# Half a gate product moved from VectorE to ScalarE and GpSimd, and a new written order for a convolution and gating kernel

## Chip, core and metric

The kernel runs on one core of a Trainium2 chip. The metric is the device time of one execution in microseconds; the median of three runs of the kernel before is 351.92 us. Engines are called PE (TensorE matmul), PEld (its weight loads), DVE (VectorE), ACT (ScalarE), POOL (GpSimd) and SP (the queue that issues most transfers).

## The reference

x has shape 8 x 4224 x 192 (batch, sequence, channel), in float32. Two stages follow each other:

```python
# stage 1: causal convolution, 7 taps, one set of softmax weights per head of 24 channels
w = softmax(weight)                       # 8 heads x 7
x = einsum('hk,bskhg->bshg', w, windows(x, 7))
# stage 2: gate and projections
gate_pre = sum(conv_w[k] * shift(x, k) for k in range(5))   # 5 taps, per channel
gate = 1 / (1 + exp(-gate_pre))
out = (gate * (x @ w_val)) @ w_out        # 192 x 192 matrices
```

## The kernel before

**Layout.** Channels lie on partitions. 192 channels are 128 + 64: chunk 1 is 128 channels of two streams side by side (tiles with `128x2x482`, on the page 964 columns), chunk 2 holds the other 64 channels of both streams in one tile of 128 partitions (482 columns). The sequence is cut into 14 groups, and these into 37 steps (0 to 36) of 288, 432, 482, 500 or 244 columns; steps 8 to 34 have 482.

**Stage 1 on PE.** A unit is 4 to 7 windows of a group: small matmuls of x with a banded weight matrix (L323, tile `pc`), whose two results ACT copies into `e` (L335); transfers then scatter rows of `e` into `x1` and `x2`, two groups ahead of use. Tiles of x come in through 8 buffers (L169).

**Stage 2 for a step n.**
- ACT writes tap 0 into an accumulator in PSUM, `pa` (chunk 1) or `pb` (chunk 2) (`gate_open`, L418); DVE adds taps 1 to 4 in place, one instruction per tap (`gate_taps`, L436); ACT writes the sigmoid into `g1` or `g2` (`gate_close`, L449). There is one `pa` and one `pb`: the next step's opening waits for this step's sigmoid.
- x is split into a rounded part `xh` and a rest `xl` (L457, L465 the casts, L458, L466 the subtractions on POOL), and PE forms the value product `v` in three banks: q = 0, 1 for chunk 1, q = 2 for chunk 2 (`diagonal` L492, `columns` L540, `rows` L529, `main` L507).
- DVE multiplies `v` by the gate (`gated`, L558), three instructions per step: two for chunk 1, one for chunk 2. The result is split again into `ph` and `pl`, PE forms the output product `o`, ACT copies it to `ot` (L574) and SP stores it.
- From step 30 on (`WHOLE`), chunk 2 is instead copied to `vt` by ACT (L746) and multiplied by POOL (L750), and parts of the products are done unsplit.

**Order.** Nothing is rearranged: each engine runs its instructions in the order in which the program writes them, and an instruction that waits holds up all behind it on its engine. The order comes from three loops (L630 to L781): steps 0 to 3, 4 to 29, and 30 to 37. In each, PE works at v of step n and o of step n-1, DVE at the taps of step n+1. The five banks for `pc`, `v` and `o` are handed out in turn, and loads of x are issued as the rows of a head are sent.

Of the kernel before, what the change touches and what calls it, by code (L numbers as in the profile page):

```python
# [24 lines left out]
NS = 5  # L25
# [66 lines left out]

UNIT = {2: 4, 3: 6, 5: 7}
# [11 lines left out]
SOON = {2: (0, 0, 1, 1), 3: (1, 2, 2, 2), 4: (3, 3, 3, 4, 4, 4), 5: (5, 5, 6, 6, 7, 7)}  # L105


@with_exitstack
def kernel(
# [21 lines left out]
    ps = ctx.enter_context(tc.tile_pool(name="ps", bufs=5, space=PSUM))  # L131
# [15 lines left out]
    xtiles, loaded = {}, [0]  # L147
# [60 lines left out]

    def zeros(k):
        pw = ps.tile([128, 512], F32, tag="p", name="pw")  # L210
        for i in range(k):
            nc.tensor.matmul(pw[:M, :ZW], lhsT=zero[:, :M], rhs=zero[:, M:], start=True, stop=True)  # L212

# [93 lines left out]
    def conv_unit(u, hold=False):  # L307
# [5 lines left out]
        if ws[0] == (0, 0):  # L313
            es[g, q] = ep.tile([M, 4 * NMAX * WIN], F32, tag="e", name=f"e_{g}_{q}")
        e = es[g, q]
        pc = [ps.tile([128, 512], F32, tag="p", name=f"pc_{u}_{r}") for r in range(2)]
        for k, (hi, j) in enumerate(ws):
# [15 lines left out]

        def evict(r):
            nc.scalar.copy(ev[:, a : a + w, r, :], pc[r][:M, : w * HW].rearrange("p (w t) -> p w t", t=HW))  # L335

        evict(0)
        if hold:
            held.append(lambda: (evict(1), send_rows(g, q, ws, e)))
        else:  # L340
            evict(1)
            send_rows(g, q, ws, e)

    held = []

    def release():
        for f in held:
            f()
        held.clear()

    def send_rows(g, q, ws, e):
        n = NJS[g]
        done = [hi for hi, j in ws if j == n - 1]
        for hi in done:
            h = QUADS[q][hi]
            i, at = home[g, h]
            last = at == len(loads[i][1]) - 1
            if last and g >= BY_POOL:
                load_x(allowed(i))
            scatter(g, h, e[:, hi * n * WIN : (hi + 1) * n * WIN])  # L360
            if last and g < BY_POOL:
                load_x(allowed(i))

    def scatter(g, h, e):
# [11 lines left out]
        def rows(c0, c1):  # L376
            return e[c0 * NS : c1 * NS, :]

        def send(dst, c0, c1, a, b, dma=dma):
            w = NS * (b - a)  # L380
            dma(dst[:, :w].rearrange("p (s t) -> p s t", s=NS), rows(c0, c1)[:, a:b])
# [22 lines left out]
    accs, g1s, g2s, xs, pr, ots, banks, sums = {}, {}, {}, {}, {}, {}, {}, {}  # L404
# [48 lines left out]
    def split1(pool, tag, n, x):  # L453
        m = STEPS[n][2]
        h = pool.tile([128, 2, MB], F32R, tag="h", name=f"{tag}h_{n}")[:, :, :m]
        l = pool.tile([128, 2, MB], F32R, tag="l", name=f"{tag}l_{n}")[:, :, :m]
        nc.scalar.copy(h, x)  # L457
        nc.gpsimd.tensor_tensor(out=l, in0=x, in1=h.bitcast(F32), op=ALU.subtract)  # L458
        return h, l

    def split2(pool, tag, n, x, copy=nc.scalar.copy):
        m = STEPS[n][2]
        h = pool.tile([128, MB], F32R, tag="h2", name=f"{tag}h2_{n}")[:, :m]
        l = pool.tile([128, MB], F32R, tag="l2", name=f"{tag}l2_{n}")[:, :m]
# [394 lines left out]
```

## Time and profile before

| | us |
|---|---|
| three runs, median (lowest, highest) | 351.92 (350.58, 352.64) |
| the profiled execution: its time | 352.94 |
| the profiled execution: its span | 350.8 |
| busy in the span: PE, DVE, ACT, POOL | 336.4, 320.4, 311.0, 252.8 |

The span is what the profiler saw of the core; the time has 2.1 us around it. Busy time of PE is modelled and counts overlapped instructions once. An instruction's duration reaches to its last write, and the next one on the engine may start a little before that, so the distance between two starts can be less than a duration. A name in brackets behind a row says how long the engine stood idle before it and what it waited for.

### The profile page before, as it was taken

To read this page: it belongs to the slowest core of one execution; us is meant where nothing else is said; L and a number is where in the kernel's file an instruction comes from. 1 tells how busy PE (TensorE), PEld (TensorE's weight loads), DVE (VectorE), ACT (ScalarE), POOL (GpSimd) and SP (SyncE) were. 2 spreads that over 40 slices of the span, in tenths; PEclk is the share of its full clock that TensorE was granted. 3 is DMA by queue.
4 is the path that set the end of the run, shared out by engine and by line. 5 is a ranking of instruction groups with operands and counts; after the bars stand their busy time and mean duration, and the time that the engine had idled before them with its cause. 6 is when DMAs were issued, how large, how long until landed. Compare 5 with 4: busy or idle time off the path is not lost.

```text
span 350.8 us, 12959 instructions
## 1 busy us (share of the span) xinstructions
PE 336.4 (96%) x5334; PEld 210.9 (60%) x5334; DVE 320.4 (91%) x427; ACT 311.0 (89%) x544; POOL 252.8 (72%) x195
## 2 busy tenths in 40 slices
PE   8778998999999999999999999999999999999995
PEld 7756655766666666666666666666666665533343
DVE  3898988898999999999999999999999998999950
ACT  7478989787998999999999999999999999999842
POOL 1859855676877888888888888887887877755551
PEclk9999999899999999999999999999999999999998
DMA  7889879899898898898798798798898783442223
GB/s 249 268 212 277 245 235 284 228 274 287 252 277 295 244 295 258 241 277 273 227 283 277 207 286 299 208 283 290 219 293 267 202 314 120 169 152 117 85 86 130
DMA packets 38947, 83.19 MB, mean 237 GB/s; under 512 B 4936, under 2 KB 17008, under 8 KB 38888
## 3 DMA queue, kind: packets, MB, share of 16 engines
q1 hardware_dynamic: 37440, 80.64, 74.9%
q0 software_dynamic: 896, 1.27, 1.5%
q8 instruction: 42, 0.69, 0.9%
q10 hardware_dynamic: 552, 0.46, 0.5%
q14 instruction: 17, 0.14, 0.1%
HBM read 30.06 MB, written 26.00 MB: 160 GB/s over the span
## 4 chain that ended last, share of the span: by engine, by line
PE 84%; DMA 4%; ACT 3%; issue 3%; DVE 2%; SPq 2%; POOL 1%; ACTq 0%; DVEq 0%; POOLq 0%
PE o L507 14%; PE pc L323 14%; PE v L507 11%; PE v L540 9%; PE o L540 8%; PE o L529 6%; PE v L492 6%; PE v L529 5%; PE o L492 5%; DMA x<-e 3%; PE v L500 2%; PE o L521 2%; PE v L521 2%; PE pw L212 1%; DVE pa L436 1%
## 5 line engine op out<-in xcount | busy, mean ns | idle before, releaser
L436 DVE SCALAR_TENSOR_TENSOR pa<-x,cwt,pa 128x964 f32<-128x964 f32 (+4 forms) x148 | 173.4, 1172 | 5.4 <-ACT pa L418 4.9
L458 POOL TENSOR_TENSOR pl<-g,ph 128x964 fp32r<-128x964 f32 (+4 forms) x37 | 79.5, 2150 | 72.1 <-ACT ph L457 63.6
L436 DVE SCALAR_TENSOR_TENSOR pb<-x,cwt,pb 128x482 f32<-128x482 f32 (+4 forms) x142 | 98.6, 694 | 0.3
L558 DVE TENSOR_TENSOR g<-v,g 128x482 f32<-128x482 f32 (+4 forms) x105 | 63.5, 630 | 10.4 <-ACT g L449 3.9
L574 ACT COPY ot<-o 128x482 f32<-128x482 f32 (+4 forms) x111 | 59.7, 547 | 14.7 <-PE o L507 10.2
L323 PE MATMUL pc<-band,x 64*64 64x58 f32 (+1 forms) x3776 | 66.5, 220 | 5.0 <-issue 1.8
L323 PEld LDWEIGHTS pc<-band,x 64*56 64x56 f32 (+1 forms) x3776 | 60.8, 132 | 17.1 <-issue 11.0
L458 POOL TENSOR_TENSOR xl<-x,xh 128x964 fp32r<-128x964 f32 (+2 forms) x32 | 64.3, 2009 | 1.7 <-ACT xh L457 1.6
L335 ACT COPY e<-pc 120x348 f32<-120x348 f32 (+2 forms) x148 | 61.7, 473 | 3.8 <-PE pc L323 3.8
L418 ACT ACTIVATE pa<-x,cwt 128x964 f32<-128x964 f32 (+4 forms) x37 | 38.1, 1029 | 2.7 <-issue 1.6
L457 ACT CAST ph<-g 128x964 fp32r<-128x964 f32 (+4 forms) x37 | 35.8, 966 | 3.8 <-DVE g L558 3.8
L466 POOL TENSOR_TENSOR xl<-x,xh 128x482 fp32r<-128x482 f32 (+2 forms) x30 | 34.2, 1139 | 5.6 <-ACT xh L465 3.6
L449 ACT ACTIVATE g<-pa 128x964 f32<-128x964 f32 (+4 forms) x37 | 34.9, 944 | 3.7 <-DVE pa L436 3.3
L492 PE MATMUL v<-x,wvf 64*64 64x482 f32 (+4 forms) x148 | 37.5, 553 | 0.0
L540 PE MATMUL v<-x,wvf 128*64 128x482 f32 (+4 forms) x148 | 37.4, 572 | 0.0
L492 PE MATMUL o<-g,wof 64*64 64x482 f32 (+4 forms) x148 | 36.5, 567 | 0.8 <-ACT e L335 0.8
L540 PE MATMUL o<-g,wof 128*64 128x482 f32 (+4 forms) x148 | 35.5, 547 | 0.0
L466 POOL TENSOR_TENSOR pl<-g,ph 128x482 fp32r<-128x482 f32 (+2 forms) x30 | 35.2, 1172 | 0.0
L507 PE MATMUL o<-ph,woh 128*128 128x482 f32 (+4 forms) x74 | 31.3, 422 | 0.2 <-ACT ph L457 0.2
L457 ACT CAST xh<-x 128x964 fp32r<-128x964 f32 (+2 forms) x32 | 31.2, 974 | 0.0
L507 PE MATMUL o<-pl,woh 128*128 128x482 f32 (+4 forms) x74 | 27.8, 376 | 1.5 <-POOL pl L458 1.5
L507 PE MATMUL o<-ph,wol 128*128 128x482 f32 (+4 forms) x74 | 27.3, 369 | 0.0
(79 smaller groups left out, 482.8 us busy)
## 6 DMA issues: line engine op xcount, KB each, us to landing
x<-xw SPq DMA_DIRECT2D x72, 300.0 KB
out<-ot SPq DMA_DIRECT2D x27, 723.0 KB
x<-e SPq DMA_DIRECT2D x45, 271.9 KB
x<-xw SPq DMA_DIRECT2D x16, 360.0 KB
x<-e SPq DMA_DIRECT2D x36, 135.9 KB
out<-ot SPq DMA_DIRECT2D x6, 648.0 KB
x<-e SPq DMA_DIRECT2D x20, 163.1 KB
x<-e SPq DMA_DIRECT2D x18, 90.6 KB
```

The lines of the kernel that those rows point to most:

```text
L323: nc.tensor.matmul(pc[r][c0:c1, k * HW : (k + 1) * HW], lhsT=xtiles[i][p, c + c0 : c + c1], rhs=band[p, 4 * q + hi, :], start=True, stop=True,
L335: nc.scalar.copy(ev[:, a : a + w, r, :], pc[r][:M, : w * HW].rearrange("p (w t) -> p w t", t=HW))
L436: nc.vector.scalar_tensor_tensor(out=acc, in0=views(n, k)[i], scalar=cwt[:, i, k : k + 1], in1=acc, op0=ALU.mult, op1=ALU.add,)
L457: nc.scalar.copy(h, x)
L458: nc.gpsimd.tensor_tensor(out=l, in0=x, in1=h.bitcast(F32), op=ALU.subtract)
L466: nc.gpsimd.tensor_tensor(out=l, in0=x, in1=h.bitcast(F32), op=ALU.subtract)
L492: nc.tensor.matmul(dst, lhsT=w22, rhs=x[HALVES[r]], start=True, stop=False)
L507: nc.tensor.matmul(acc, lhsT=a[:, r], rhs=b[:, q], start=(fresh and i == 0), stop=(not fresh and i == 2))
L529: nc.tensor.matmul(acc, lhsT=a[p, r], rhs=b[p], start=(fresh and i == 0), stop=(not fresh and i == 2))
L540: nc.tensor.matmul(acc[HALVES[q if what == "v" else 1 - q]], lhsT=w.f[:, W12 : W12 + 64], rhs=x[:, q], start=False, stop=True)
L558: nc.vector.tensor_tensor(out=v, in0=banks.pop(("v", n, q)), in1=v, op=ALU.mult)
L574: nc.scalar.copy(ots[n][:, q * m : (q + 1) * m], banks.pop(("o", n, q)))
```

## The change

Four things are changed.

1. **Chunk 2 divided by columns.** In steps 6 to 29 DVE multiplies only the left columns of chunk 2 (`gate_left`, token `gd`: 241 of 482, in two steps 216 of 432). ACT copies the right columns of the bank to `vt` (`copy_part`, `vp`), and POOL multiplies them by the gate (`gate_right`, `gq`). As built, the DVE half waits for ScalarE alone, and reads the same bank that the copy reads.
2. **The three loops are replaced by a table.** `ORDER` has a string of tokens for each step; a token is one instruction or a small group, `+1` or `-1` says that it is for the next or the last step, and `A` and `B` are the next tap of `pa` and `pb`. Steps 10 to 25 have one pattern but for the place of the loads of x.
3. **Loads of x** after the start are tokens of their own (`x`), and evictions of `pc` (`e10` and so on) are too. The five banks are taken from a list, the longest free first.
4. **Casts change engine**: in most steps `ph2` is now cast on POOL and `xh2` on ACT; a few of the casts `ph` and `xh` early and late go to POOL. In the whole program ACT has 24 part copies more and 25 casts less, POOL 24 half products and 25 casts more. The numbers of PE, DVE and transfer instructions are the same. `EVEN = 99` leaves `cut` at 64 everywhere, so the windows' matmuls have the shapes of before.

```diff
+SHARE = 241
+ORDER = (
...
+    """
+    dv e11-1 x x ph-1 c2-1 xh2+1 co-1 e20-1 A A e21-1 x pl2-1 cv sB o2-1 ro-1 pl-1 vp gq rv gd A oB+1 B mv0
+    mo0-1 g0 xh+1 mv1 B xl+1 g1 mo1-1 ph2P sA+1 o0-1 oA+2 B xl2+1 o1-1 c1 do e10 A B
+    """,
...
-    ps = ctx.enter_context(tc.tile_pool(name="ps", bufs=5, space=PSUM))
+    ps = ctx.enter_context(tc.tile_pool(name="ps", bufs=1, space=PSUM))
...
+    free = [ps.tile([128, 512], F32, tag=f"p{i}", name=f"p_{i}") for i in range(5)]
+    def take(key):
+        taken[key] = free.pop(0)
+        return taken[key]
+    def give(key):
+        free.append(taken.pop(key))
...
+    def high(p, n, c, copy):
...
+        copy(two[0], x)
+        hs[p, n, c] = x, two
+    def low(p, n, c):
+        x, (h, l) = hs.pop((p, n, c))
         nc.gpsimd.tensor_tensor(out=l, in0=x, in1=h.bitcast(F32), op=ALU.subtract)
...
+    def split_v(n):
+        m = STEPS[n][2]
+        return m - min(SHARE, m // 2)
+    def leave_v(n, other):
+        if (other, n) in did:
+            drop("v", n, 2)
+    def copy_part(n):
+        a = split_v(n)
+        vts[n] = vp.tile([128, MB], F32, tag="vt", name=f"vt_{n}")[:, : STEPS[n][2] - a]
+        nc.scalar.copy(vts[n], banks["v", n, 2][:, a:])
+        leave_v(n, "gd")
+    def gate_left(n):
+        a = split_v(n)
+        v = g2s[n][:, :a]
+        nc.vector.tensor_tensor(out=v, in0=banks["v", n, 2][:, :a], in1=v, op=ALU.mult)
+        leave_v(n, "vp")
+    def gate_right(n):
+        v = g2s[n][:, split_v(n) :]
+        nc.gpsimd.tensor_tensor(out=v, in0=vts.pop(n), in1=v, op=ALU.mult)
...
+    for n, tokens in enumerate(ORDER):
+        for t in tokens.split():
+            if t in "AB":
+                tap(t)
+                continue
+            if t == "x":
+                load_x(loaded[0] + 1)
+                continue
+            i = max(t.rfind("+"), t.rfind("-"))
+            step(t[:i] if i > 0 else t, n + (int(t[i:]) if i > 0 else 0))
```

Three places show what moves. The first is DVE in the middle of the program, one step's worth; `pa_18` is the accumulator of chunk 1 of step 18, `g2_18` the gate of chunk 2, and two names with different last numbers are different tiles. Before, from the second half of step 18:

```order
L436 SCALAR_TENSOR_TENSOR pb_18_3151<-x2_7_2312,cwt_158,pb_18_3151 128x482
L436 SCALAR_TENSOR_TENSOR pa_19_3203<-x1_7_2311,cwt_158,pa_19_3203 128x2x482
L436 SCALAR_TENSOR_TENSOR pb_18_3151<-x2_7_2312,cwt_158,pb_18_3151 128x482
L436 SCALAR_TENSOR_TENSOR pa_19_3203<-x1_7_2311,cwt_158,pa_19_3203 128x2x482
L558 TENSOR_TENSOR g2_18_3297<-v_18_2_3283,g2_18_3297 128x482
L436 SCALAR_TENSOR_TENSOR pa_19_3203<-x1_7_2311,cwt_158,pa_19_3203 128x2x482
L436 SCALAR_TENSOR_TENSOR pb_19_3304<-x2_7_2312,cwt_158,pb_19_3304 128x482
L436 SCALAR_TENSOR_TENSOR pa_19_3203<-x1_7_2311,cwt_158,pa_19_3203 128x2x482
L436 SCALAR_TENSOR_TENSOR pb_19_3304<-x2_7_2312,cwt_158,pb_19_3304 128x482
L558 TENSOR_TENSOR g1_18_3201<-v_18_0_3337,g1_18_3201 128x482
L558 TENSOR_TENSOR g1_18_3201<-v_18_1_3338,g1_18_3201 128x482
```

Now, the step before it (`p_0` to `p_4` are the five banks):

```order
L597 SCALAR_TENSOR_TENSOR pa_18_2908<-x1_7_2194,cwt_162,pa_18_2908 128x2x482
L597 SCALAR_TENSOR_TENSOR pb_17_2880<-x2_7_2195,cwt_162,pb_17_2880 128x482
L597 SCALAR_TENSOR_TENSOR pa_18_2908<-x1_7_2194,cwt_162,pa_18_2908 128x2x482 x2
L725 TENSOR_TENSOR g2_17_2998<-p_0_121,g2_17_2998 128x241
L597 SCALAR_TENSOR_TENSOR pa_18_2908<-x1_7_2194,cwt_162,pa_18_2908 128x2x482
L597 SCALAR_TENSOR_TENSOR pb_18_3020<-x2_7_2195,cwt_162,pb_18_3020 128x482
L699 TENSOR_TENSOR g1_17_2905<-p_3_124,g1_17_2905 128x482
L597 SCALAR_TENSOR_TENSOR pb_18_3020<-x2_7_2195,cwt_162,pb_18_3020 128x482
L699 TENSOR_TENSOR g1_17_2905<-p_2_123,g1_17_2905 128x482
```

The product of chunk 2 is half as wide; the two products of chunk 1 stand apart with a tap between them; and two taps of the same `pa` stand next to each other (`x2`), where before a tap of `pb` or a product always stood between two taps of one accumulator.

The second place is ACT in the same stretch. Before:

```order
L449 ACTIVATE g1_17_3054<-pa_17_2905 128x2x482
L418 ACTIVATE pa_18_3056<-x1_7_2311,cwt_158 128x2x482
L335 COPY e_8_1_2952<-pc_44_0_3066 120x7x58
L335 COPY e_8_1_2952<-pc_44_1_3067 120x7x58
L335 COPY e_8_1_2952<-pc_45_0_3101 120x6x58
L457 CAST ph_16_3138<-g1_16_2903 128x2x482
L449 ACTIVATE g2_17_3142<-pb_17_3004 128x482
L335 COPY e_8_1_2952<-pc_45_1_3102 120x6x58
L418 ACTIVATE pb_18_3151<-x2_7_2312,cwt_158 128x482
L457 CAST xh_18_3157<-x1_7_2311 128x2x482
L574 COPY ot_16_3166<-o_16_2_3131 128x482
L465 CAST ph2_17_3168<-g2_17_3142 128x482
```

Now, up to the sigmoid that ends `pa` of the next step:

```order
L503 COPY e_8_1_2814<-p_1_122 120x7x58
L624 CAST ph_16_2953<-g1_16_2761 128x2x482
L624 CAST xh2_18_2980<-x2_7_2195 128x482
L503 COPY e_8_1_2814<-p_4_125 120x6x58
L503 COPY e_8_1_2814<-p_3_124 120x6x58
L610 ACTIVATE g2_17_2998<-pb_17_2880 128x482
L736 COPY ot_16_3000<-p_2_123 128x482
L719 COPY vt_17_3009<-p_0_121 128x241
L579 ACTIVATE pb_18_3020<-x2_7_2195,cwt_162 128x482
L624 CAST xh_18_3030<-x1_7_2194 128x2x482
L610 ACTIVATE g1_18_3045<-pa_18_2908 128x2x482
```

The cast `ph2` has left ACT and `xh2` has come; the part copy `vt` stands behind the sigmoid of `g2` and an output copy, and it is what the half product of `g2_17` on DVE waits for.

The third place is DVE in step 1. Before:

```order
L436 SCALAR_TENSOR_TENSOR pa_1_440<-x1_0_179,cwt_158,pa_1_440 128x2x288
L436 SCALAR_TENSOR_TENSOR pb_1_478<-x2_0_180,cwt_158,pb_1_478 128x288 x2
L558 TENSOR_TENSOR g2_1_602<-v_1_2_606,g2_1_602 128x288
L436 SCALAR_TENSOR_TENSOR pa_2_598<-x1_1_298,cwt_158,pa_2_598 128x2x432
L558 TENSOR_TENSOR g1_1_596<-v_1_0_620,g1_1_596 128x288
```

Now:

```order
L597 SCALAR_TENSOR_TENSOR pa_1_428<-x1_0_183,cwt_162,pa_1_428 128x2x288
L597 SCALAR_TENSOR_TENSOR pb_1_464<-x2_0_184,cwt_162,pb_1_464 128x288
L699 TENSOR_TENSOR g2_0_462<-p_2_123,g2_0_462 128x288
L597 SCALAR_TENSOR_TENSOR pb_1_464<-x2_0_184,cwt_162,pb_1_464 128x288
L699 TENSOR_TENSOR g1_1_595<-p_1_122,g1_1_595 128x288
L699 TENSOR_TENSOR g1_1_595<-p_0_121,g1_1_595 128x288
L699 TENSOR_TENSOR g2_1_627<-p_3_124,g2_1_627 128x288
```

Between the last tap of `pb_1` and the product that needs its sigmoid, `g2_1`, there was nothing; now two products stand there.

## Rows read from the trace of the kernel before

**Rows 1.** The page: busy us, share of the span and instructions of each engine.
```profile
PE 336.4 (96%) x5334; PEld 210.9 (60%) x5334; DVE 320.4 (91%) x427; ACT 311.0 (89%) x544; POOL 252.8 (72%) x195
```
**Rows 2.** Stretches: length, then busy PE, PEld, DVE, ACT, POOL; clock; DMA.
```profile
17.00:111.00 94.00, 86.62 (x1612) 57.86 (x1612) 85.02 (x116) 82.37 (x153) 67.99 (x60) 0.98 0.89 258
111.00:290.00 179.00, 179.00 (x3029) 114.63 (x3030) 179.00 (x224) 170.34 (x284) 143.36 (x100) 1.00 0.87 264
290.00:337.00 47.00, 46.97 (x350) 20.66 (x346) 42.82 (x52) 43.69 (x73) 29.36 (x19) 1.00 0.32 115
```
**Rows 3.** Timeline of DVE over one step: start us, length us, instruction, count.
```profile
181.41 1.25 DVE L558 TENSOR_TENSOR g<-v,g 128x482 f32<-128x482 f32 x2
...
186.15 0.65 DVE L558 TENSOR_TENSOR g<-v,g 128x482 f32<-128x482 f32 x1
186.72 1.22 DVE L436 SCALAR_TENSOR_TENSOR pa<-x,cwt,pa 128x964 f32<-128x964 f32 x1
187.85 0.72 DVE L436 SCALAR_TENSOR_TENSOR pb<-x,cwt,pb 128x482 f32<-128x482 f32 x1
...
190.28 0.66 DVE L558 TENSOR_TENSOR g<-v,g 128x482 f32<-128x482 f32 x1
```
**Rows 4.** Timeline of DVE late: three taps of one accumulator in a row.
```profile
301.70 3.75 DVE L436 SCALAR_TENSOR_TENSOR pa<-x,cwt,pa 128x964 f32<-128x964 f32 x3
```
**Rows 5.** Groups by form: busy us, mean ns of one, idle before.
```profile
L558 DVE TENSOR_TENSOR g<-v,g 128x482 f32<-128x482 f32 x76 | 48.0, 658 | 2.2 <-PE v L507 1.8 <-PE o L540 0.3
...
L574 ACT COPY ot<-o 128x244 f32<-128x244 f32 x3 | 1.1, 363 | 1.2 <-PE o L507 0.7 <-PE o L540 0.4
...
L558 DVE TENSOR_TENSOR g<-v,g 128x244 f32<-128x244 f32 x3 | 1.2, 412 | 2.9 <-ACT g L449 1.8 <-PE v L500 1.1
```
**Rows 6.** Timeline of ACT over one step in the middle.
```profile
190.01 0.98 ACT L449 ACTIVATE g<-pa 128x964 f32<-128x964 f32 x1
191.03 1.07 ACT L418 ACTIVATE pa<-x,cwt 128x964 f32<-128x964 f32 x1
192.04 1.19 ACT L335 COPY e<-pc 120x348 f32<-120x348 f32 x3
193.11 1.01 ACT L457 CAST ph<-g 128x964 fp32r<-128x964 f32 x1
194.02 0.57 ACT L449 ACTIVATE g<-pb 128x482 f32<-128x482 f32 x1
194.49 0.49 ACT L335 COPY e<-pc 120x406 f32<-120x406 f32 x1
...
196.36 0.57 ACT L574 COPY ot<-o 128x482 f32<-128x482 f32 x1
196.81 0.61 ACT L465 CAST ph<-g 128x482 fp32r<-128x482 f32 x1
```
**Rows 7.** Who waited for whom, DVE: us in total, times, longest.
```profile
DVE pa L436 <- ACT pa L418: 4.9, 6, 1.6
DVE g L558 <- ACT g L449: 3.9, 6, 1.8
DVE g L558 <- PE v L507: 2.8, 5, 1.5
```
**Rows 8.** Timeline of DVE in step 1, the place shown above.
```profile
28.25 1.08 DVE L436 SCALAR_TENSOR_TENSOR pb<-x,cwt,pb 128x288 f32<-128x288 f32 x2
30.41 0.46 DVE L558 TENSOR_TENSOR g<-v,g 128x288 f32<-128x288 f32 x1 [1.08 <-ACT g L449]
```
**Rows 9.** Timeline of PE: windows and the next `columns`, middle, then late.
```profile
190.75 1.68 PE L323 MATMUL pc<-band,x 64*64 64x58 f32 x102
...
193.49 1.03 PE L540 MATMUL v<-x,wvf 128*64 128x482 f32 x4
...
305.93 0.92 PE L323 MATMUL pc<-band,x 64*64 64x58 f32 x48
...
307.73 1.03 PE L540 MATMUL v<-x,wvf 128*64 128x482 f32 x4
```

More of the change, by code (lines that the diff above doesn't have):

```diff
@@ L91, with cut @@
 PER_LOAD = {2: 2, 3: 2, 5: 1}
+EVEN = 99
+SHARE = 241
+def cut(g, h):
+    return M // 2 if g >= EVEN and h < 5 else 64
 UNIT = {2: 4, 3: 6, 5: 7}
@@ L313, in conv_unit @@
         if ws[0] == (0, 0):
[L314 to L316 removed]
+            es[g, q] = ep.tile([128, 4 * NMAX * WIN], F32, tag="e", name=f"e_{g}_{q}")
+        pc = [take(("c", u, r)) for r in range(2)]
         for k, (hi, j) in enumerate(ws):
@@ L615 @@
     gate_open(0, 1)
-    split(0)
+    high("x", 0, 2, nc.scalar.copy)
+    low("x", 0, 2)
+    high("x", 0, 1, nc.scalar.copy)
+    low("x", 0, 1)
     gate_taps(0, 0, 1, 2)
@@ L781, with tap @@
-    assert not held
+    by_order.append(True)
+    unit_of = {}
+    u = done[0]
+    for n in range(N):
+        unit_of[n] = list(range(u, min(u + todo[n], len(units))))
+        u += len(unit_of[n])
+    assert u == len(units)
+    line = {
+        c: [(n, k) for n in range(1, N) for k in range(2 if i and n in SUMMED else 1, KG)]
+        for i, c in enumerate("AB")
+    }
+    def tap(c):
+        if line[c]:
+            n, k = line[c].pop(0)
+            gate_taps(n, "AB".index(c), k, k + 1)
@@ new lines, in evicts, with step @@
+    def evicts(n, i, r):
+        if i <= len(unit_of[n]):
+            evict(unit_of[n][i - 1], r)
+    def step(t, n):
+        copy = nc.gpsimd.tensor_copy if t[-1] == "P" else nc.scalar.copy
+        t = t.removesuffix("P")
+        p, c = t[0], 2 if t[-1] == "2" else 1
+        assert ok(n) and (t, n) not in did, (t, n)
+        did.add((t, n))
+        if t in ("dv", "do"):
+            diagonal(t[1], n)
+        elif t in ("cv", "co"):
+            columns(t[1], n)
+        elif t in ("rv", "ro"):
+            rows(t[1], n)
+        elif p == "m":
+            main(t[1], n, int(t[2]))
+        elif p == "c":
+            if int(t[1]) <= len(unit_of[n]):
+                conv_unit(unit_of[n][int(t[1]) - 1])
+        elif p == "e":
+            evicts(n, int(t[1]), int(t[2]))
+        elif t in ("g0", "g1", "g2"):
+            gated(n, int(t[1]))
+        elif t == "vp":
+            copy_part(n)
+        elif t == "gd":
+            gate_left(n)
+        elif t == "gq":
+            gate_right(n)
+        elif t == "vt":
+            copy_v(n)
+        elif t == "gp":
+            gate_v(n)
+            did.add(("g2", n))
+        elif t in ("o0", "o1", "o2"):
+            project(n, int(t[1]))
+        elif p == "s" and t != "su":
+            gate_close(n, "AB".index(t[1]))
+        elif t in ("oA", "oB"):
+            gate_open(n, "AB".index(t[1]))
+        elif t == "su":
+            gate_sum(n)
+        elif p in "xp" and (n < PLAIN if p == "x" and c == 1 else n < WHOLE or c == 1):
+            if t[1] == "h":
+                high(p, n, c, copy)
+            else:
+                low(p, n, c)
```

434 lines of the change are left out of this document (204 added, 230 removed).

## The prediction

> **What bounds the kernel now.** I read the busy shares first [rows 1]: PE 96%, DVE 91%, ACT 89%. A share is a mean over stages, so the stretches came next [rows 2]. From 111 to 290 us PE and DVE are busy for all of the 179.00 us; ACT stands idle for 8.66, POOL for 35.64. From 17 to 111 DVE is idle for 94.00 - 85.02 = 8.98 us and PE for 7.38. From 290 to 337 PE is full again (46.97 of 47.00) and DVE idle for 4.18. PE's clock is 0.98 to 1.00 throughout, so it does not enter.
>
> Which of two full engines sets the pace? The timeline of DVE over one step [rows 3] tells it from starts: the pair of products starts at 181.41 and the next at 190.28, so a step takes 8.87 us and no start is late. A product takes 186.72 - 186.15 = 0.57 us to the next start, a tap of `pa` 187.85 - 186.72 = 1.13. PE is hardly looser. From the start of a step's windows to `columns` it takes 193.49 - 190.75 = 2.74 us for 102 passes [rows 9]; late it takes 307.73 - 305.93 = 1.80 for 48. At the rate of the 102 (1.68 us, 16 ns a pass) 54 passes fewer are 0.89 us less, which makes 1.85: at most about 0.1 us of a step on PE is waiting. So a faster DVE can win only some 0.1 us per step before PE takes over, unless PE's own order gets shorter.
>
> **The change part by part.** All numbers of instructions are counted in the two orders.
>
> *Halved products.* A product of 482 columns lasts 658 ns and one of 244 lasts 412 [rows 5]: 1.03 ns a column. 241 columns fewer save 0.25 us, so the start-to-start time falls from 0.57 to 0.32. There are 22 of these and two with 216 columns fewer (0.22): 5.9 us less on DVE.
>
> *Taps of one accumulator side by side.* Three taps of `pa` in a row last 3.75 us in all [rows 4]; without the last one's 1.23 that is 1.26 from start to start, 0.13 more than the 1.13 of a tap that something else follows. A tap reads what the one before it wrote, and beside its neighbour nothing covers the end of that write. Before, 15 pairs of `pa` taps stand so, now 49: 34 x 0.13 = 4.4 us more. Pairs of `pb` go from 9 to 12, which at the same 0.13 is 0.4. DVE therefore keeps only 5.9 - 4.8 = 1.1 us of work less, spread unevenly. Steps 10 to 27 have one such pair each and one halved product: 0.25 - 0.13 = 0.12 us per step. The late steps, from 28, have 7 + 5 pairs more and two halved products: 1.1 us more. Steps 0 to 9 come out even.
>
> *Middle.* By DVE a step falls from 8.87 to 8.75. ACT must still fit. It is busy 170.34 of 179.00 us, which is 8.44 of each 8.87. The part copy adds 0.25 (half of 482 columns at 1.03, the 363 ns of a 244-column copy [rows 5] being the bound above); the casts that change places are equal in size. That makes 8.69. POOL has room: 143.36 of 179.00. A halved product on DVE now stands behind ACT's part copy; queued behind it on DVE are the last tap of `pa`, and so the next sigmoid on ACT. The ring this closes, in starts from [rows 6]: sigmoid 1.02, output copy 0.45, opening 1.01, output copy 0.45, four evictions of 0.36 (three from 192.04 to 193.11), cast `ph` 0.91, cast `xh2` at most 0.61, sigmoid of `g2` 0.47, output copy 0.45, part copy 0.36: 7.17 on ACT; then 0.32 and one tap of 1.22 on DVE: 8.71. It fits by 0.04. Three engines within 0.1 us of one another will not all meet their best, so I take 0.10 of the 0.12: 18 steps give 1.8 us.
>
> *Early.* What DVE waits for is mostly ACT [rows 7]: reopened accumulators 4.9 us, sigmoids 3.9, v products 2.8, in the whole run. In step 1 two taps of `pb` are followed at once by the product that needs the sigmoid of that `pb`: 1.08 us idle [rows 8]. The new order puts two products between. From the last tap of `pa` to the first of the next step it now has six instructions instead of three in step 1, three for two in step 2, four for two in step 3. Such waits can be hidden; the longest, 1.6 us, comes when a new group's data are first used, and order alone does not bring those sooner. What goes is between nothing and 7.4 us, since PE idles for no more than that there and has no work less. The waits that got longer cover are nearer to half than to either end: I take 3.4 us.
>
> *Late.* DVE's 1.1 us lie within its 4.18 us of idle, and PE is full: nothing. If that cover is gone, 1.1 us.
>
> *Loads and evictions as tokens, banks from a list.* In the middle a tile of x is still issued about five heads ahead and its buffer was freed some heads ago; the work of those heads hides it. Were it late, PE would wait for it as single windows may anywhere. I cost it at nothing.
>
> Sum: 1.8 + 3.4 = 5.2 us. The profiled execution took 352.94 (span 350.8 and 2.1 around it), which gives 347.7. It stands 1.0 above the median of the runs, 351.92; against that the forecast is 346.7.
>
> **Rivals.**
>
> *A, the waits really go (slack everywhere).* The taps' neighbourhood costs nothing because the copy or a product's end was the true limit there, and PE's second windows block hides its `diagonal`. Then a middle step loses all of 0.25, 18 x 0.25 = 4.5, and early all of PE's 7.4: 11.9 us, 340.0. For it: PE's late steps are shorter than the middle ones [rows 9]. Against it: the 1.26 was read where DVE had no other work.
>
> *B, PE is the bound and the early waits only move.* PE's 179.00 of 179.00 speaks for it, and each early wait on a new group comes back elsewhere. Then the middle gives nothing and early at most 1.5: 350.4 to 352.5, about 351.5.
>
> *C, slower: the halved product waits for the part copy.* The place is the product of chunk 2 on DVE in each of the 18 middle steps. DVE has two taps, 1.26 + 1.13 = 2.39 us, between the last tap of `pb` and this product; ACT must do a sigmoid, an output copy and the part copy in them (0.47 + 0.45 + 0.36 = 1.28), but five older instructions stand ahead on ACT. It decides as soon as the ring is over 8.87. The ring has 8.71 without any stall, and ACT's present idle is 8.66 us in 179.00, 0.43 per step; if that stays inside the ring it is 9.14, 0.27 per step over before: 4.9 us more in the middle, with half of the early gain, 1.7, against it: 355.1. Were nothing on ACT overlapped, more still; but [rows 6] shows starts 0.1 us ahead of ends throughout.
>
> The Trainium skill (PSUM — Partial Sum Buffer, section PSUM bank collisions raise a hardware error) speaks for this wait: two engines that touch the same bank and the same 32 partitions at once collide, reads against reads too. By it the two halves cannot be read side by side, and the wait of the one for the other cannot be taken out of the order. No run here shows a collision; by the rule the price would be C's, without it the product would wait only for the sigmoid and C's chance would fall.
>
> **How the numbers follow.** The forecast has 0.52: between the middle at 0.05 and at 0.15 per step and early at 1 to 6 us it reaches from 343.5 to 350.5. A has 0.13, B 0.19, C 0.16. The range for 8 in 10 leaves out the low half of A and the upper part of C: 341 to 354.5. About 0.5% (1.8 us) is what a measurement of this kernel tells from no change, so faster means under 350.2 and slower over 353.7. Faster: 0.50 + 0.13 + a little of B, 0.65. Same: most of B and the edges of the others, 0.21. Slower: most of C, 0.14.
>
> **What would show it.** DVE's busy time should fall by about 1 us, not 6, and pairs of `pa` taps in the middle should start 1.26 apart; 1.13 would speak for A. The step in the middle, from one pair's place to the next, should be 8.75 to 8.8. Idle of DVE from 17 to 111 us should fall from 8.98 to between 4 and 6. C would show as DVE idle before the 241-column product, with ACT's copy as what ended it, in nearly every step. B would show as DVE idle before products of chunk 1 with PE as what ended it. The forecast is wrong if the middle step stays at 8.87, or if early idle does not fall.

## The result and the profile after

The changed kernel took 347.19 us (median of 346.73, 347.06, 347.31 and 349.42), the kernel before 351.61 beside it: a ratio of 0.987, with an interval from 0.983 to 0.991. Two later series gave 348.25 (0.990, 0.986 to 0.994) and 348.40 (0.986, 0.983 to 0.990). Medians here and below leave out the few slow executions, over 1.5% longer than the fastest of the same kernel; the profile of the third series is of such a one and is not used. Forecast were 346.7, with 341 to 354.5 as the range. The profiled execution took 347.06, span 345.3, against 352.94 and 350.8 before: 5.5 us less span.

The page after: busy us, share and instructions, answering to [rows 1], and the chain of work that ended last, by engine (PE had 84% of it before).

```profile
PE 335.5 (97%) x5334; PEld 215.0 (62%) x5334; DVE 316.2 (92%) x427; ACT 298.9 (87%) x543; POOL 284.4 (82%) x244
...
PE 93%; ACT 2%; DMA 1%; SPq 1%; DVE 1%; issue 1%; DVEq 0%
```

DVE's busy time fell by 4.2 us, where the prediction had about 1. The same three stretches as in [rows 2], in the same columns:

```profile
17.00:111.00 94.00, 90.96 (x1728) 59.86 (x1730) 87.21 (x120) 74.84 (x144) 82.82 (x80) 0.96 0.89 265
111.00:290.00 179.00, 178.90 (x2944) 118.69 (x2941) 176.10 (x223) 174.16 (x305) 158.71 (x124) 1.00 0.85 263
290.00:337.00 47.00, 47.00 (x353) 20.48 (x351) 41.45 (x53) 37.05 (x63) 32.38 (x23) 1.00 0.32 121
```

Early, DVE's idle time fell from 8.98 to 6.79 us and PE's from 7.38 to 3.04, with a lower clock (0.96). In the middle PE is as full as before, but DVE is now idle for 2.90 us. Late, PE is full in both.

Where the 5.5 us came from is read from the openings of `pa` on ACT, one in each step. From that of step 0 to that of step 10 it took 101.63 - 16.84 = 84.79 us before and 98.03 - 16.16 = 81.87 after (2.9 less); from step 10 to 27, 151.39 and 149.78 (1.6 less); from 27 to the end 97.78 and 97.49 (0.3 less); the first opening came 0.7 earlier. Of the first three, the prediction had 3.4, 1.8 and nothing; the fourth it did not have. The early part divides further: steps 0 to 5 took 40.45 before and 40.31 after, steps 5 to 10 took 44.34 and 41.55, so nearly all of the 2.9 lies in the second half.

One step of DVE in the middle, which answers to [rows 3] and [rows 4]:

```profile
172.39 2.48 DVE L597 SCALAR_TENSOR_TENSOR pa<-x,cwt,pa 128x964 f32<-128x964 f32 x2
174.90 0.41 DVE L725 TENSOR_TENSOR g<-p,g 128x241 f32<-128x241 f32 x1
175.23 1.22 DVE L597 SCALAR_TENSOR_TENSOR pa<-x,cwt,pa 128x964 f32<-128x964 f32 x1
...
181.12 2.48 DVE L597 SCALAR_TENSOR_TENSOR pa<-x,cwt,pa 128x964 f32<-128x964 f32 x2
183.73 0.41 DVE L725 TENSOR_TENSOR g<-p,g 128x241 f32<-128x241 f32 x1
```

Two taps of `pa` side by side last 2.48, which is 1.26 to the second and 1.22 for it. The halved product takes 175.23 - 174.90 = 0.33 to the next start. But it does not start 1.13 after the second tap (which would be 174.78 and 183.51): it is 0.12 and 0.22 late. ACT over the same stretch, answering to [rows 6], shows why:

```profile
176.48 0.98 ACT L610 ACTIVATE g<-pa 128x964 f32<-128x964 f32 x1
...
178.79 0.57 ACT L736 COPY ot<-p 128x482 f32<-128x482 f32 x1
179.43 0.90 ACT L503 COPY e<-p 120x406 f32<-120x406 f32 x2
...
182.84 0.59 ACT L736 COPY ot<-p 128x482 f32<-128x482 f32 x1
183.28 0.41 ACT L719 COPY vt<-p 128x241 f32<-128x241 f32 x1
...
185.31 0.98 ACT L610 ACTIVATE g<-pa 128x964 f32<-128x964 f32 x1
```

The part copy ends at 183.28 + 0.41 = 183.69, and the product starts at 183.73. From sigmoid to sigmoid it is 8.83 us, the ring of the prediction (8.71), with one gap in it: the eviction at 179.43 starts 0.64 after the output copy where 0.45 is usual, since it waits for PE. In the second profile this eviction starts 0.05 after the end of PE's windows in all 14 steps from 13 to 26, and 0.06 to 0.19 later than the output copy in front of it would let it. So the ring of the prediction has room left in each step; what holds the step runs through PE. DVE's waits, answering to [rows 7]:

```profile
DVE g L699 <- PE p L695: 4.4, 2, 3.6
...
DVE g L725 <- ACT vt L719: 1.0, 4, 0.4
...
DVE pa L597 <- ACT pa L579: 0.7, 3, 0.3
```

The waits for reopened accumulators went from 4.9 to 0.7 us. A new one, of 3.56 us, stands before the product of chunk 2 of step 0:

```profile
30.49 0.46 DVE L699 TENSOR_TENSOR g<-p,g 128x288 f32<-128x288 f32 x1 [3.56 <-PE p L695]
```

### The profile page after: what moved, and what is told of

It reads as the page before. It is cut to its first block, busy times and chain, and to the rows that moved or that the text cites. A ratio compares the mean times of both kernels' runs of the same rounds, so it can differ in the third digit from the quotient of the medians.

```text
span 345.3 us, 13001 instructions
## 1 busy us (share of the span) xinstructions
PE 335.5 (97%) x5334; PEld 215.0 (62%) x5334; DVE 316.2 (92%) x427; ACT 298.9 (87%) x543; POOL 284.4 (82%) x244
## 4 chain that ended last, share of the span: by engine, by line
PE 93%; ACT 2%; DMA 1%; SPq 1%; DVE 1%; issue 1%; DVEq 0%
PE p L666 27%; PE p L695 18%; PE p L487 17%; PE p L686 14%; PE p L653 10%; PE p L678 3%; PE p L659 2%; PE p L375 1%; DMA x<-xw 1%; SPq L538 1%; ACT e L503 1%; DVE pa L597 1%; ACT g L610 0%; DVE pb L597 0%; ACT pa L579 0%
## 5 line engine op out<-in xcount | busy, mean ns | idle before, releaser
L629 POOL TENSOR_TENSOR pl<-g,ph 128x482 fp32r<-128x482 f32 (+5 forms) x67 | 114.6, 1722 | 11.9 <-ACT ph L624 8.6
L629 POOL TENSOR_TENSOR xl<-x,xh 128x964 fp32r<-128x964 f32 (+5 forms) x62 | 98.0, 1584 | 17.1 <-ACT xh L624 12.4
L487 PEld LDWEIGHTS p<-band,x 64*56 64x56 f32 (+1 forms) x3776 | 67.7, 133 | 30.9 <-ACT e L503 8.9
L487 PE MATMUL p<-band,x 64*56 64x58 f32 (+1 forms) x3776 | 73.4, 220 | 4.8 <-issue 1.5
L503 ACT COPY e<-p 120x348 f32<-120x348 f32 (+2 forms) x148 | 63.3, 478 | 9.6 <-PE p L487 8.7
L736 ACT COPY ot<-p 128x482 f32<-128x482 f32 (+4 forms) x111 | 60.1, 550 | 11.7 <-PE p L695 4.0
L699 DVE TENSOR_TENSOR g<-p,g 128x482 f32<-128x482 f32 (+4 forms) x81 | 49.4, 620 | 12.7 <-PE p L695 4.4
L624 ACT CAST xh<-x 128x964 fp32r<-128x964 f32 (+5 forms) x48 | 39.2, 818 | 0.0
L653 PE MATMUL p<-g,wof 64*64 64x482 f32 (+4 forms) x148 | 37.3, 556 | 0.0
L653 PE MATMUL p<-x,wvf 64*64 64x482 f32 (+4 forms) x148 | 37.3, 569 | 0.0
```

Source lines behind the costliest of these rows:

```text
L487: nc.tensor.matmul(pc[r][64 * s : 64 * s + c1 - c0, k * HW : (k + 1) * HW], lhsT=xtiles[i][p, c + c0 : c + c1], rhs=band[p, 4 * q + hi, :] ...
L503: nc.scalar.copy(ev[:, a : a + w, r, :], taken["c", u, r][:me, : w * HW].rearrange("p (w t) -> p w t", t=HW))
L624: copy(two[0], x)
L653: nc.tensor.matmul(dst, lhsT=w22, rhs=x[HALVES[r]], start=True, stop=False)
L699: nc.vector.tensor_tensor(out=v, in0=drop("v", n, q), in1=v, op=ALU.mult)
L736: nc.scalar.copy(ots[n][:, q * m : (q + 1) * m], drop("o", n, q))
```

## Experiments

"Step" is the mean step in the middle: the time from the opening of `pa` in step 13 to that in step 27, by 14. The ratio is to the kernel before, which ran beside each (medians 351.6 to 352.5). On PE a step has four stretches, each counted from its first start to the first start of the next: the windows with the `diagonal` matmuls, the `columns`, the `rows`, and the passes of `main`. The `columns` take 1.77 and the passes 2.81 to 2.83 in every kernel (but for one stall, below); the means of the other two over the same 14 steps are in the last columns.

| kernel | median us | ratio, 95% interval | steps 0 to 10 | step | windows, diagonals | rows |
|---|---|---|---|---|---|---|
| before | 351.6 | 1 | 84.79 | 8.856 | 2.76 | 1.51 |
| changed | 347.19 | 0.987, 0.983 to 0.991 | 81.87 | 8.784 | 2.54 | 1.60 |
| changed, second series | 348.25 | 0.990, 0.986 to 0.994 | 81.26 | 8.719 | 2.54 | 1.58 |
| changed, third series | 348.40 | 0.986, 0.983 to 0.990 | | | | |
| product whole | 349.59 | 0.995, 0.991 to 0.998 | 80.59 | 8.855 | 2.66 | 1.61 |
| halves only | 363.37 | 1.033, 1.029 to 1.038 | 85.05 | 9.389 | 2.85 | 1.95 |
| halves only, earlier copy | 354.10 | 1.005, 1.001 to 1.008 | 84.88 | 8.945 | 2.85 | 1.51 |
| more pairs | 354.17 | 1.007, 1.005 to 1.010 | 82.52 | 8.991 | 2.76 | 1.64 |
| part copy earlier | 352.81 | 1.003, 1.000 to 1.005 | 82.83 | 9.069 | 2.54 | 1.93 |
| output copy first | 347.39 | 0.988, 0.985 to 0.992 | 83.94 | 8.664 | 2.57 | 1.51 |
| and cast later | 346.49 | 0.985, 0.983 to 0.988 | 82.36 | 8.639 | 2.54 | 1.51 |
| and cast later, again | 346.96 | 0.985, 0.981 to 0.990 | 82.15 | 8.748 | 2.55 | 1.61 |
| loads back | 350.01 | 0.996, 0.993 to 1.000 | 84.67 | 8.730 | 2.53 | 1.61 |
| cast later, first loads by count | 346.12 | 0.981, 0.976 to 0.986 | 82.37 | 8.640 | 2.54 | 1.51 |

The first profile of the changed kernel holds a lone stall between the openings of steps 16 and 17 (9.22 us; four `columns` of PE took 1.69 in place of 0.98); the second has none, and its step is 8.72, so the middle really gives 0.14 a step, 2.3 to 2.5 us. The second profile with the cast later holds one too, of 1.5 us in PE's rows of one step: without it its step would be 8.64 as well.

**The product whole, in the new order.** In all rows:

```diff
- ... sB o2-1 ro-1 pl-1 vp gq rv gd A oB+1 B mv0
+ ... sB o2-1 ro-1 pl-1 rv g2 A oB+1 B mv0
```

> The changed kernel with the product of chunk 2 whole on DVE again and without the part copy; its written order is kept. Theory (DVE and PE both lie within 0.1 us of the step, so DVE's 0.25 us a step decides): a middle step goes from 8.81 to about 9.0, and the time to 351 to 353 us, 4 to 6 more than the changed kernel. Rival 1 (PE or the ring through ACT sets the step, so DVE's work is free): at most 1.5 us more than the changed kernel, under 349. Rival 2 (the new order alone is what made it faster, and the part copy only costs): faster than the changed kernel.

2.4 us slower than the changed kernel's first series (1.3 than the second), the step at 8.855: less than the 9.0 and the 351 to 353 us of the theory, more than the first rival. DVE over one step:

```profile
183.49 0.66 DVE L699 TENSOR_TENSOR g<-p,g 128x482 f32<-128x482 f32 x1
184.05 1.22 DVE L597 SCALAR_TENSOR_TENSOR pa<-x,cwt,pa 128x964 f32<-128x964 f32 x1
...
189.95 2.48 DVE L597 SCALAR_TENSOR_TENSOR pa<-x,cwt,pa 128x964 f32<-128x964 f32 x2
192.34 0.65 DVE L699 TENSOR_TENSOR g<-p,g 128x482 f32<-128x482 f32 x1
```

The pair and the product behind it run without a gap (192.34 - 189.95 = 2.39 = 1.26 + 1.13): here DVE sets the step, and its work is 8.85 with a pair in it. So it was 8.85 - 0.13 = 8.72 in the kernel before, not 8.87, and is 8.85 - 0.24 = 8.61 in the changed one. The new order alone, with its loads, gives nothing in the middle, and all of the early gain (80.59).

**More pairs, in the old order.** Steps 5 to 29:

```diff
-        taps("AABAA" if n == HEAD else "ABAB")
+        taps("AABAA" if n == HEAD else "AABB")
```

> The kernel before with four taps of steps 5 to 29 written A A B B in place of A B A B: the same work, one more pair of neighbouring taps of pa and one of pb per step. Theory (a tap behind a tap of the same accumulator starts 0.13 us later, and DVE sets the step): 0.13 to 0.23 us a step, 3 to 6 us slower than before, 355 to 358; pairs of pa 1.26 apart. Rival (the 0.13 is hidden, since DVE is not what sets the step): within 1 us of before.

2.5 us slower, between the theory (3 to 6) and the rival (within 1); the step rose by 0.135.

```profile
186.12 2.48 DVE L436 SCALAR_TENSOR_TENSOR pa<-x,cwt,pa 128x964 f32<-128x964 f32 x2
187.38 1.23 DVE L436 SCALAR_TENSOR_TENSOR pa<-x,cwt,pa 128x964 f32<-128x964 f32 x1
188.51 1.48 DVE L436 SCALAR_TENSOR_TENSOR pb<-x,cwt,pb 128x482 f32<-128x482 f32 x2
189.90 1.22 DVE L558 TENSOR_TENSOR g<-v,g 128x482 f32<-128x482 f32 x2
```

The second tap starts 1.26 after the first, and the two of `pb` take 1.39 where two apart take 0.63 each: 0.13 for each pair. That is 0.26 of added work a step for 0.135 of added time. The other half fell into waits of the kernel before that its profile does not list. Three more rows of the step in [rows 3], on DVE of the kernel before:

```profile
188.47 1.22 DVE L436 SCALAR_TENSOR_TENSOR pa<-x,cwt,pa 128x964 f32<-128x964 f32 x1
189.60 0.72 DVE L436 SCALAR_TENSOR_TENSOR pb<-x,cwt,pb 128x482 f32<-128x482 f32 x1
...
192.14 1.23 DVE L436 SCALAR_TENSOR_TENSOR pa<-x,cwt,pa 128x964 f32<-128x964 f32 x1
```

The tap of `pb` at 187.85 [rows 3] has its follower 0.62 later; the one at 189.60 has the pair of products only 0.68 later, at 190.28. Such a wait of 0.05 lies within the 0.72 that the tap counts as busy. The second place is the first tap of the next `pa`, at 192.14: it starts 0.03 after ACT's opening of that `pa` ends (191.03 + 1.07 = 192.10 [rows 6]), and so it does in all 15 middle steps. Against the shortest distance seen for the same two kinds of instruction, the pair of products is 0.04 late in the mean, this tap 0.07, and three other starts 0.01 each: 0.14 a step.

**Halves only.** The kernel before with the products of steps 6 to 29 cut, the copy behind the opening of `pb` (shortened):

```diff
+        columns("v", n)
...
+        vt = ...; nc.scalar.copy(vt, acc[:, a:])
+        nc.vector.tensor_tensor(out=g[:, :a], in0=acc[:, :a], in1=g[:, :a], op=ALU.mult)
+        nc.gpsimd.tensor_tensor(out=g[:, a:], in0=vt, in1=g[:, a:], op=ALU.mult)
         split(n + 1)
-        columns("v", n)
-        gated(n, 2)
```

> The kernel before with only the products of chunk 2 of steps 6 to 29 cut by columns between DVE and POOL; its order, its loads and its taps stay. Theory (PE takes over within about 0.1 us): a middle step goes from 8.87 to 8.75 or 8.80, 24 steps give 2 to 3 us, the time is 349 to 350. Rival (DVE alone sets the step, rival A of the prediction): 0.25 a step, 6 us, 346. Rival (the halved product waits for the copy on ACT, rival C): slower than before, over 353.

11.7 us slower: rival C, in the old order, at twice its price (0.53 a step, where the prediction had 0.27). DVE's waits and two steps of its timeline:

```profile
DVE g L722 <- ACT vt L720: 19.8, 24, 1.2
```
```profile
182.23 0.41 DVE L722 TENSOR_TENSOR g<-v,g 128x241 f32<-128x241 f32 x1 [0.78 <-ACT vt L720]
...
191.64 0.41 DVE L722 TENSOR_TENSOR g<-v,g 128x241 f32<-128x241 f32 x1 [0.84 <-ACT vt L720]
```

24 waits in 24 steps, 0.8 us each: the product stands in a ring with the last tap of `pa`, the sigmoid and the rest of ACT's queue.

**Halves only, earlier copy.** As before, the block of the copy moved between `close()` and `release()`, behind the sigmoid of `pb`:

```diff
+        columns("v", n)
+        vt = ...; (copy and both halves as above)
         release()
         reopen()
-        columns("v", n)
```

> The kernel before with only the products of chunk 2 of steps 6 to 29 cut by columns, as in the run with halves only, but with the part copy two places earlier on ACT, straight behind the sigmoid of pb, so that the product need not wait 0.8 us for it. Theory A (DVE's own work sets the step of the kernel before, as the prediction had it): a middle step of 8.62 to 8.70, the whole 348 to 349. Theory B (a ring sets it: output copies, sigmoid and opening of pa and the eviction behind them on ACT, the bank that this eviction frees, and PE's diagonal, columns, rows and o passes up to the output copies again): DVE gets emptier and the step stays at 8.86, the whole within 1.5 us of before.

The long wait is gone and DVE has 0.25 us a step less to do, yet the step is 0.09 longer than before, and the time 1.7: theory A failed, and B had the step at 8.86.

```profile
181.73 1.25 DVE L558 TENSOR_TENSOR g<-v,g 128x482 f32<-128x482 f32 x2 [0.15 <-PE v L507]
```

Now the wait for PE is long enough to be listed. This run alone does not tell what set the step of the kernel before, since the copy is new work on ACT. The trace of the kernel before does: the waits in its middle stretch, rows of ACT and of PE in the step of [rows 6] and [rows 9], and a row of ACT behind them:

```profile
ACT ot L574 <- PE o L507: 6.2, 20, 0.4
```
```profile
192.04 0.45 ACT L335 COPY e<-pc 120x348 f32<-120x348 f32 x1
```
```profile
192.23 0.65 PE L492 MATMUL v<-x,wvf 64*64 64x482 f32 x2
192.54 0.62 PE L492 MATMUL o<-g,wof 64*64 64x482 f32 x2
...
197.32 0.38 PE L507 MATMUL o<-pl,woh 128*128 128x482 f32 x1
```
```profile
197.73 1.21 ACT L574 COPY ot<-o 128x482 f32<-128x482 f32 x2 [0.31 <-PE o L507]
```

The ring closes link by link. The first output copy starts when PE's passes of that o end (197.32 + 0.38 = 197.70); behind the two copies stand the sigmoid of `pa`, its opening and the evictions, with no gap over 0.04; and when the first eviction ends (192.04 + 0.45 = 192.49), PE's `diagonal` of o starts. From there to the passes of o PE takes no longer than in any other kernel. In all 14 steps from 13 to 26 the copies start 0.04 after the end of their passes, the opening 0.03 after the end of the sigmoid, and the `diagonal` of o 0.05 after the end of the eviction. There PE stands still: the `diagonal` of o comes 0.14 to 0.27 (0.20 in the mean) behind that of v. In the new order the two start together, as in these rows of the changed kernel (`x,wvf` is that of v, `g,wof` that of o), and the windows and diagonals take 2.54 in place of 2.76:

```profile
179.12 0.61 PE L653 MATMUL p<-x,wvf 64*64 64x482 f32 x1
179.12 0.57 PE L653 MATMUL p<-g,wof 64*64 64x482 f32 x1
```

So a ring through ACT and PE set the step of the kernel before, and DVE waited on it. No edit cut this ring by itself.

It also explains the 0.09 of this run. From the sigmoid of `pb` to the eviction behind it on ACT it is now 0.61 + 0.26 = 0.87 us (185.54, 186.15, 186.41) in place of 0.47, which is 0.40 more; 0.31 of it is what ACT waited for PE before, and its waits no longer list that.

**The part copy earlier, in the new order.** Rows 10 to 26:

```diff
- ... cv sB o2-1 ro-1 pl-1 vp gq rv gd ...
+ ... cv sB vp o2-1 ro-1 pl-1 gq rv gd ...
```

> The changed kernel with the part copy of chunk 2 one place earlier on ACT, ahead of an output copy, in the 17 like steps (10 to 26). Theory (the wait of the 241-column product for this copy, 0.13 to 0.2 us a step, is slack that PE would fill): the wait in front of the product goes, PE shows the time instead, and the whole is 0 to 1 us less than the changed kernel. Rival (the ring through ACT sets the step): 0.1 us a step, 1.5 to 2 us less, 345.5 or under.

Both theories failed: about 5 us slower, the step at 9.069. The wait before the halved product stayed (0.14 us in the median), a product of chunk 1 now waits too (0.2 us, 16 times), and PE waits besides. First ACT, then PE's rows of x, then one of the waits from 111 to 290 us, all of this kernel:

```profile
177.48 0.36 ACT L719 COPY vt<-p 128x241 f32<-128x241 f32 x1
177.74 0.57 ACT L736 COPY ot<-p 128x482 f32<-128x482 f32 x1
```
```profile
178.04 0.80 PE L686 MATMUL p<-xh,wvh 64*128 64x482 f32 x2
```
```profile
PEld p L686 <- ACT ot L736: 6.8, 18, 0.8
```

The output copy that now stands behind the part copy frees the bank which these rows write. It ends at 178.31, and the rows, which take 0.38 when nothing holds them, take 0.80. All of the 0.35 that a step lost stands in PE's rows (1.93 in place of 1.58); 0.26 of it is what the copy was moved by, the rest was not traced. So a second ring closes in the changed kernel: eviction, casts, evictions, sigmoid and output copy on ACT, then rows, passes and windows on PE up to the next eviction. In the changed kernel itself it costs 0.07, since its rows take 1.58 where 1.51 is enough.

**The output copy first.** The opposite move, rows 10 to 26; in the second kernel the cast `xh2` of the next step is taken out of both rings as well (first diff, then the new line of the second):

```diff
- ... c2-1 xh2+1 co-1 ... cv sB o2-1 ro-1 pl-1 vp gq rv gd A oB+1 B mv0
+ ... c2-1 xh2+1 co-1 ... cv o2-1 sB ro-1 pl-1 vp gq rv gd A oB+1 B mv0
```
```diff
+ ... c2-1 co-1 ... cv o2-1 sB ro-1 pl-1 vp gq rv gd A oB+1 xh2+1 B mv0
```

> The changed kernel with the output copy of chunk 2 one place earlier on ACT, ahead of the sigmoid of pb, in the 17 like steps (10 to 26). Theory (a ring through ACT's output copy, which frees the bank that PE's next rows need, sets the step or nearly does, as the run with the copy one place later showed): PE gets its bank 0.45 us earlier, the eviction of the first unit of windows no longer waits for PE (0.13 to 0.19 us a step), and the step falls from 8.78 to about 8.70, the other ring through the part copy; 1 to 1.5 us less in the whole. Rival (PE's own work fills the step): nothing changes, within 0.5 us of the changed kernel.

> As the run with the output copy first, and the cast of chunk 2 of x for the next step moved on ACT behind the opening of pb, out of the ring from the sigmoid of pa through the part copy and the halved product back to that sigmoid. Theory (two rings through ACT set the step): both rings are now near 8.25, and the step falls to the work of the fullest engine, 8.62 to 8.70 (DVE has 8.62, ACT 8.57); 1.5 to 2.5 us less than the changed kernel in the whole. Rival 1 (PE's own work fills the step): as the changed kernel, 8.78. Rival 2 (the cast comes too late for the low part on POOL and the rows on PE that use it): slower.

> The changed kernel once more, beside the others of this call: 346.7 to 349.5 us, and a middle step (from the opening of pa in step 13 to that in step 27) of 8.78 us.

The step fell to 8.664 and 8.639, as the theory of the two rings had it. Rows of x on PE with the output copy first:

```profile
178.34 0.38 PE L686 MATMUL p<-xh,wvh 64*128 64x482 f32 x2
```

No row of PE is drawn out any more. With both edits all four of PE's stretches are at the lowest seen in any of the kernels (2.54, 1.77, 1.51 and 2.82, in sum 8.64): as far as these runs show, PE's own work sets the step here, and DVE (8.61) is 0.03 under it. So PE's work fills the step after all, not at the 8.78 of the rival but at 8.64. The changed kernel beside them had 8.72 and not the 8.78 expected, which came from the profile with the stall. In the whole, the first edit does not stand out: its profile lost 2 us before step 10, where the edit begins. The second was 1.8 us under the changed kernel, and again:

> The kernel with the output copy first and the cast later, once more beside the changed kernel: 346 to 347 us, 0.3 to 0.6% under the changed kernel, a middle step of 8.64; or, if the gain in the steps is too small to be seen in the whole, within 0.3% of it.

> The changed kernel beside it: 347 to 348.5 us, a middle step of 8.72 to 8.78.

346.96 against 348.40, 1.4 less; the steps agree with that (0.08 x 17 = 1.4), but the intervals of the ratios (0.981 to 0.990 and 0.983 to 0.990) overlap, so by the whole time alone it is not settled.

**Loads back.** The changed kernel with its loads by count of finished heads, as before the change (shortened; `last` marks the last head that needs a tile of x):

```diff
+            if last and g >= BY_POOL:
+                load_x(allowed(i))
             scatter(g, h, e[:, hi * n * WIN : (hi + 1) * n * WIN])
-            if at == len(loads[i][1]) - 1 and not by_order:
+            if last and g < BY_POOL:
                 load_x(allowed(i))
...
-    by_order.append(True)
...
             if t == "x":
-                load_x(loaded[0] + 1)
                 continue
```

> The changed kernel with its loads of x issued where the kernel before issues them, by the count of finished heads, in place of their own places in the written order. Theory (the place of the loads costs and gives nothing, as the prediction had it): within 1 us of the changed kernel. Rival (the new places of the loads make part of the early gain): 1 to 4 us slower than the changed kernel, with waits of PE for x from 17 to 111 us.

1.8 us slower by the medians, 2.4 by the ratios, though the two intervals touch. In the profile steps 0 to 10 take 84.67, as before the change: the whole early gain is gone. ACT and DVE at the opening of step 8:

```profile
83.51 1.07 ACT L582 ACTIVATE pa<-x,cwt 128x964 f32<-128x964 f32 x1 [3.75 <-DMA x<-e]
```
```profile
84.61 1.23 DVE L600 SCALAR_TENSOR_TENSOR pa<-x,cwt,pa 128x964 f32<-128x964 f32 x1 [2.93 <-DMA x<-xw]
```

The convolved rows that the opening reads land late; with loads placed one by one the same opening is not held (from the opening of step 7 to that of step 8 it is 12.35 us here, 10.32 before the change, 8.65 in the changed kernel). This is more than one profile: steps 5 to 10 take 41.5 to 41.6 us in all seven profiles with placed loads, and 43.6 to 47.0 with loads by count, three of them in the old order, this one and the next in the new. One run by count is an exception: more pairs, 41.86. So loads by count can be in time, but mostly are not. Steps 0 to 5 were faster here (37.7 us against 39.1 to 42.5 with placed loads), hence:

**The first rows' loads by count.** The kernel with the cast later, its loads by count in rows 0 to 4 and by the order from row 5.

> The kernel with the output copy first and the cast later, and with the loads of x of its first five rows (steps 0 to 4) issued by the count of finished heads, as the kernel before does; from row 5 on each load has its own place in the order. Theory (the new places of the loads pay from step 5 to step 10, where the run with all loads back lost 5.4 us, and cost some 2.5 us from step 0 to step 5, where it took 37.7 us against 39 to 40): 37.7 us for steps 0 to 5, 41.5 for steps 5 to 10, and the whole 2 to 3 us less than without this edit, 344 to 345. Rival (the difference in the first five steps is chance from one profile to the next, with the arrival of the first loads and the clock): 346 to 347, as without it. Rival (the loads stand behind each other from the first rows on, so that steps 5 to 10 slow down too): 348 or more.

Steps 0 to 5 took 38.2 and steps 5 to 10 took 44.2, in sum 82.37 as without the edit (82.36 and 82.15). What the early loads give in steps 0 to 5 is lost again in steps 5 to 10: the time came as the first rival had it, but the first five steps were no chance (38.2 and 37.7 by count, never under 39.1 else); the wait only moves. Which transfers then stand in the way was not tested. At 346.12 it is the lowest median of all, but not apart from 346.49.

## Why the prediction was right in its number, and where it was not

**The bound: the step that failed.** That "a step takes 8.87 us and no start is late" was wrong. Two starts were late by 0.04 and 0.07 in the mean and three by 0.01, 0.14 in all; that is less than a row's length reaches over the next start (0.72 against 0.63), so neither the idle time nor the list of waits shows it. Two runs agree: 0.26 of work added cost 0.135, and a step truly full of DVE is 8.855 with a pair. Hence DVE's busy time fell by 4.2 and not by 1.1: some 3 us of the 320.4 were such waits. The same reading failed for PE. The estimate of "at most about 0.1 us of a step on PE" took 16 ns a pass from the length of the last pass too; the 102 passes start within 1.48 us (190.75 to 192.23), 14.5 ns each, and the late step that it was compared with waits too (the `diagonal` of o comes 0.13 behind that of v). In the middle the wait was 0.20. The Trainium skill (Perfetto Trace Analysis, section Identifying the Most-Contended Engine) tells to take the engine with the highest occupancy first and calls occupancy a fair measure for VectorE; here 179.00 of 179.00 us held 0.14 of 8.86 in waits a step, a small error, but the two runs that moved work off DVE in the old order became slower, so emptying the fullest engine by that measure was no gain by itself.

**Halved products and pairs** were right: 0.24 less a product, 1.26 for a tap beside its like, 0.13 for a pair of `pb` too.

**Middle.** The gain came out at 1.6 us (2.5 in the profile without the stall), forecast 1.8. That the size is right is luck: DVE's work is 8.61 and not 8.75, and the step does not follow it. The prediction had DVE as the limit before and after. The runs show the ring through PE's passes of o and ACT before (8.86), and after it PE's own work (8.64) with 0.07 of wait for an output copy (8.72). PE's work had room because the new order shortens its windows and diagonals by 0.22, the case that the prediction named ("unless PE's own order gets shorter") and did not work out. The ring through the part copy, worked out as 8.71 and called a fit "by 0.04", has 0.06 to 0.19 left in each step. Only both parts together gain: in the old order the halves lose (8.945 or 9.389), in the new order the whole product keeps the step at DVE's 8.855, both give 8.72.

**Early.** 2.9 and 3.5 us in two profiles, forecast 3.4, but the cause was put in the wrong place and in the wrong edit, so this number too is luck. The waits for reopened accumulators and sigmoids went, as written; yet steps 0 to 5, where the prediction counted them, gave nothing in the first profile (40.45 to 40.31) and 0.7 in the second (39.73): other waits took their place. The gain lies in steps 5 to 10, and with the loads back where they were it is gone. "I cost it at nothing" for the loads is the term that failed: it is worth some 2 to 3 us, and a new group's data, which "order alone does not bring" sooner, is what the placed loads bring. DVE's early idle time, for which the prediction had 4 to 6, was 6.79, and 94.00 - 87.92 = 6.08 in the second profile. The 1.08 us of [rows 8] went, and the 3.56 came; the wait at that product is 0.34 to 2.69 in other profiles with the same first rows. In the run with the product whole, whose first rows are the same, it is 0.64. About half of the difference is PE's clock, by an estimate: from PE's rows of x to the product it is 3.94 us here and 2.48 there. The pages of the changed kernel and of that run, then the `columns` in front of the product in the same two:

```profile
PEclk9996999999999999999999999999999999999999
```
```profile
PEclk9999999999999999999999999999999999999999
```
```profile
28.71 1.23 PE L695 MATMUL p<-x,wvf 128*64 128x288 f32 x4
```
```profile
27.03 0.71 PE L695 MATMUL p<-x,wvf 128*64 128x288 f32 x4
```

In the fourth slice (25.9 to 34.5 us) the changed kernel had 0.6 of the full clock in the mean; from 24.4 to 31.2 us it was 0.50, the lower of the two levels (1.2 of 2.4 GHz). Ahead of the fall PE paused for 0.79 and 0.63 us. The run with the product whole paused there for 1.39 and 0.52 and kept the full clock, so what made the clock fall stays open. The `columns` took 1.23 and not 0.71, and the wait of DVE 3.56 and not 0.64.

**Late:** nothing was forecast, and from step 27 on it is 0.3.

**Rivals.** A did not happen. B was right that PE bounds the kernel once DVE is emptier, and in steps 0 to 5 that the waits only move; it was wrong that nothing is won, since PE's order got shorter and the loads came sooner. C holds as a mechanism in each step read: the halved product starts 0.03 to 0.04 after the end of ACT's copy in all 14 middle steps of the second profile, up to 0.2 late. It does not set the step there, because the ring has room at the eviction. In the old order it cost 0.53 a step, twice the price that the prediction gave it, so C was real and the new order is what avoids it. That the product starts only behind the end of the copy is as the rule of the Trainium skill on collisions (PSUM — Partial Sum Buffer, section PSUM bank collisions raise a hardware error) would have it; that the two could run side by side was not tried.

## What to carry to other kernels

Work that was moved off a full engine gained only where the engine that took it had room in the same ring: write down, from one repeated step of the timeline, which start waits for which end until the ring closes, for every engine and for the banks too, before trusting busy shares. Compare starts with the shortest start-to-start time seen for the same kind of instruction, in other runs too, since waits shorter than the overlap count as busy; the stretch of an engine that is longer than its shortest is where the ring passes. And when a written order changes, give the loads their places in it and test them apart from the rest.

## What the runs showed of the hardware

A tap that adds into the accumulator which the tap before it wrote starts 0.13 us later than behind another one, for 964 columns (1.26 against 1.13) and for 482 (1.39 less 0.63 is 0.76, against 0.63) alike: for these two sizes a fixed price. The early clock differs from execution to execution of the same rows: 0.6 in one slice of 40 in the first profile of the changed kernel, full throughout with the product whole. The first five steps took between 39.1 and 42.5 us in kernels that are the same there, which is more than the two edits to the rings bring; only the repeated step tells those apart.
